# Background work of a two-stage attention and gated-MLP kernel: due times from formulas replaced by a table of places

## The chip, the cores and the metric

The kernel runs on one core of one Trainium2 chip. The metric is the device time of one execution in microseconds (us). It is stated as the median of the runs shown; a profiled execution has its own time.

## The reference

`x` has 4 batches of 12480 rows of 128 numbers; `inducing` has 32 rows. Attention is done twice, first the 32 rows over all rows of a batch, then all rows over the 32 results. What comes out goes through a two-layer network of width 2048 with a gate `h * clip(h + 3, 0, 6) / 6`.

```python
def mab(q, kv):
    s = scale * (q @ kv.transpose(0, 2, 1))
    s = s - s.max(-1, keepdims=True)
    a = np.exp(s)
    a /= a.sum(-1, keepdims=True) + 1e-09
    return a @ kv
h = mab(I, x)                      # I: inducing, once per batch
y = mab(x, h).reshape(49920, 128)
h = y @ w_in                       # 128 x 2048
out = (h * np.clip(h + 3.0, 0.0, 6.0) / 6.0) @ w_out
```

## The kernel before

The kernel doesn't carry every row through the wide network. An output row is a softmax mixture of 32 vectors, so as long as no gate saturates, the network's output is a quadratic form in the 32 softmax weights. Its coefficients are worked out once per batch from the 32 vectors. A check counts at the end whether the conditions held, and a slow direct path would run if not.

The rows of a batch are cut into 7 groups: six of 2048 rows (128 partitions x 16) and a last one of 192 rows (96 partitions x 2). A group of 2048 has four chunks of 512 rows, the last group is one chunk, so a batch has 25 chunks (`NCK`), and the four batches make 100 steps of one loop, `for t in range(total)`.

**A step** makes the output of chunk t. In order: `b_evac` of the chunk before (VectorE multiplies the PSUM tile `op` by `r_all` into `os`, L896; SyncE sends a full group to memory), `b_spread` (SyncE copies `dk` of chunk t+6 to 128 partitions as `d`), `b_prod` (VectorE makes `TD` from `TF` and `d` for chunk t+1, L846), `b_bp` and `b_TF` (TensorE makes `bp` from `xT` and `W`, L818; ScalarE its exponential `TF`, L831; two halves for chunk t+2), `b_lin` (TensorE opens `op` with the linear part from `nf` and `BD`, L857), `b_rp` and `b_r` (the row sums `rp` for t+1, L761, and their reciprocals), and four times `b_quad` (16 matmuls of 128 columns into `op` from `TF`, `TD` and `Cq`, L876).

**Work per group** makes what its chunks need: `b_pp` and `b_dk` (product `pp`, L783, exponential `dk`, L797), `b_ep` and `b_e` (`ep`, L702, and `e`), later `b_sp` and `b_nf` (`sp`, L722, on TensorE; `nf` on VectorE, L732). Before, the first four stand together at one place, seven steps ahead of the group's first chunk (the list `ahead`), and the last two together three steps ahead (`sums`).

**Background work** of the next batch runs between the quads. Phase a, per group: four casts of `xr` to `xb` (`a_cast`, L299), two times eight transposes `pt` (`a_T`, L310) and their copies to `xT` (`a_xT`, L317), scores (`a_scores`, L323), exponential `a` (`a_exp`), two aggregations `hnd` (`a_agg`, L360), and the sum `dacc` (`a_sum`); `load_x` on the queue of GpSimd (POOL) fetches a group of 1 MB into one of five buffers. Phase c: `dred`, `den`, `rD`, `H`, `htp`, `HT`, `W`, `Wd` (from the 32 vectors), `G` (`c_G3`, 48 groups of small products), copies `Gc`, then for each of 16 blocks the differences `dG` on POOL (L543 a gate that reads the latest `TD`, L545 and L546 two subtractions), their square `sq` on ScalarE (L553), and the product `C` (L641) into one long-lived PSUM tile `cp`; also `hs`, `L`, `lt`, `BD` and last `Cq`, which the next batch's quads need.

What sets the order: every engine executes its instructions in the order in which the program issues them (the scheduling is manual). Before, `a_units` and `c_units` give every unit of background work a due time in steps, worked out from weights and a few knots. A sorted `queue` is emptied by `bg` at three places in a step: after quad 0, after quad 1 and the `ahead` entries, and after quad 2. A unit can hold work of several engines: `turned(g, h)` is eight transposes and their copy, `turned(b)` of phase c runs from `htp` to `Wd`. A cast goes to POOL or to ScalarE by a rule; copies `xT` all go to VectorE in the loop. The start of the program, up to the first step, is a list written out by hand (`ORDER`).

PSUM: `bp`, `pp`, `ep`, `sp`, `rp`, `pt`, `s`, `dps`, `htp`, `gp`, `cp`, `lp` and `lt` share five banks (`psF`); `op` has two, `hnd` one. A product that finds no free bank waits until ScalarE or VectorE has read one out.

Of the kernel before, what the change touches and what calls it, by code (L numbers as in the profile page):

```python
# [24 lines left out]
TG = 16  # L25
SL = 4
# [4 lines left out]
CASTLEAD = 1.6  # L31
SUMG = 5
BY_DVE = (2, 6, 11)


# [32 lines left out]
def kernel(  # L68
# [40 lines left out]
    with ExitStack() as es:  # L109
# [44 lines left out]
        held = []  # L154
# [7 lines left out]

        def load_next(b, g):

            if b == 0:
                if g > NGR - XBUF:
                    held.append(g - (NGR - XBUF))
            elif g < XBUF and g + XBUF < NGR:
                load_x(b, g + XBUF)
            elif b + 1 < B:  # L170
                load_x(b + 1, g - (NGR - XBUF))

# [111 lines left out]
        S = {}  # L284

        def a_begin(b):
            S.setdefault(b, {})["dacc"] = cst.tile([P, TG * M], FP32, name="dacc")
# [13 lines left out]
        def a_T(b, g, h, how="f"):  # L301
            t0, p, n = groups[g]
            st = S[b]
            lo, hi = (0, n // 2) if h == 0 else (n // 2, n)
            xb = xbs[(b, g)]
            if h == 0:
                st[("xT", g)] = (xTp if n == TG else xTl).tile([P, n * p], BF16, name="xT")
            pt = bank(how, [P, 1024], BF16, "pt")
            for i in range(lo, hi):
                nc.tensor.transpose(pt[:, (i - lo) * p : (i - lo + 1) * p], xb[:p, i, :], ident_b[:p, :p])  # L310
            st[("pt", g, h)] = pt

        def a_xT(b, g, h, eng):
            t0, p, n = groups[g]
            lo, hi = (0, n // 2) if h == 0 else (n // 2, n)
            pt = S[b].pop(("pt", g, h))
            eng(S[b][("xT", g)][:, lo * p : hi * p], pt[:, : (hi - lo) * p])  # L317
# [35 lines left out]
        def a_agg(b, g, h):  # L353
# [13 lines left out]
            if h and (b, g) != (1, 0):  # L367
                load_next(b, g)
# [9 lines left out]

        def a_units(b, when):

            us = []
            cum = [0.0]

            def put(w, fn, lead=0.0):
                us.append((cum[0], lead, fn))
                cum[0] += w

            def cast(g, h):
                own = h < 2 and when(late_from[g] / cum[0]) >= (b - 1) * NCK
                a_cast(b, g, ((nc.gpsimd.tensor_copy if own else nc.scalar.copy, h, h + 1),))  # L390

            def turned(g, h):
                a_T(b, g, h)
                a_xT(b, g, h, nc.vector.tensor_copy)

            def weighed(g):
                a_scores(b, g)
                a_exp(b, g)

            def summed(g, h):  # L400
                a_agg(b, g, h)
                if h == 0:
                    a_sum(b, g)

            late = []
            late_from = {}
            for g in range(NGR):
                late_from[g] = cum[0]
                k = 1.0 if groups[g][2] == TG else 0.2
                gap = 0.46 * k + (0.49 if late else 0.0)  # L410
                if g == 0 and b > 1:
                    us.append((0.0, CASTLEAD + 0.1, lambda: a_begin(b)))
                if (b, g) == (1, 0):
                    put(0.46 * 2 + 0.2 + 0.5, lambda: None)
                else:
                    for h in range(4):
                        us.append((cum[0] + gap * (h // 2), CASTLEAD - 0.4 * (h % 2), lambda g=g, h=h: cast(g, h)))
                    put(0.46 * k, lambda g=g: turned(g, 0))
                    if late:
                        put(0.49, late.pop(0))  # L420
                    put(0.46 * k, lambda g=g: turned(g, 1))
                    if late:
                        put(0.49, late.pop(0))
                    else:
                        put(0.2, lambda: None)
                    put(0.5 * k, lambda g=g: weighed(g))
                late = [lambda g=g: summed(g, 0), lambda g=g: summed(g, 1)]
                if (b, g) == (1, 0):
                    late = [lambda: load_next(1, 0), lambda: None]
            put(0.4, lambda: None)  # L430
            put(0.1, late[0])
            put(0.1, late[1])
            return [(when(w / cum[0]) - lead, fn) for w, lead, fn in us]
# [225 lines left out]
        def c_units(b, t0, t1):  # L659

            us = []

            def put(at, fn):
                us.append((at, fn))

            def turned(b):
                c_htp(b)
                c_HT(b)
                c_HTb(b, nc.vector.tensor_copy)
                c_HTl(b)  # L670
                c_W(b)
                c_Wd(b)

            put(t0, lambda: c_sum(b))
            put(t0 + 0.9, lambda: (c_den(b), c_rD(b), c_H(b), c_d(b)))
            put(t0 + 1.6, lambda: turned(b))
            put(t0 + 2.7, lambda: c_G3(b, 0, 4))
            put(t0 + 3.05, lambda: c_G3(b, 4, 8))
            put(t0 + 3.4, lambda: c_G3(b, 8, 12))
            put(t0 + 3.75, lambda: (c_G3(b, 12, 16), c_Gcopy(b, 0)))  # L680
            put(t0 + 4.1, lambda: (c_Gcopy(b, 1), c_dG(b, 0), c_dG(b, 1)))
            tb = t0 + 5.0
            pace = (t1 - 1.0 - tb) / FB
            for jb in range(FB):
                at = tb + jb * pace
                put(at, lambda jb=jb: (c_sqG(b, jb), c_dG(b, jb + 2) if jb + 2 < FB else None))
                put(at + 0.99, lambda jb=jb: c_C(b, jb))
            put(t0 + 5.0, lambda: c_hs(b))
            put(tb + 6.5 * pace, lambda: c_L(b, 0))
            put(tb + 7.5 * pace, lambda: (c_L(b, 1), c_Lcopy(b)))  # L690
            put(tb + 10.5 * pace, lambda: (c_lt(b), c_BD(b)))
            put(t1, lambda: c_tail(b))
            return us

# [137 lines left out]

        def b_base(b, c, k):
            b_bp(b, c, k)
            b_TF(b, c, k)
# [219 lines left out]
        queue = []  # L1055

        def bg(at):
            while queue and queue[0][0] <= at:
                queue.pop(0)[1]()

        plan = []

        for b in range(1, B):
            z = (b - 1) * NCK
            knots = {
                1: [(0.0, -3.0), (0.092, -1.0), (0.093, 0.7), (1.0, 9.0)],
                2: [(0.0, z - NCK + 9.5), (0.75, z), (1.0, z + 4.5)],
            }.get(b, [(0.0, z - NCK + 6.0), (0.9, z), (1.0, z + 2.5)])

            def when(f, knots=knots):  # L1070
                for (f0, t0), (f1, t1) in zip(knots, knots[1:]):
                    if f <= f1:
                        break
                return t0 + (t1 - t0) * (f - f0) / (f1 - f0)

            hi = knots[-1][1]
            plan += a_units(b, when)
            plan += c_units(b, hi + 0.4, z + NCK - 1.0)
        queue += sorted(plan, key=lambda u: u[0])
        a_begin(0)  # L1080
        S[1] = {}
# [11 lines left out]
        ahead, sums = {}, {}  # L1093
        for b in range(B):
            for g in range(NGR):
                t = b * NCK + first_chunk[g]
                ahead.setdefault(t - AHEAD - 1, []).append(lambda b=b, g=g: (b_pp(b, g), b_dk(b, g), b_ep(b, g), b_e(b, g)))
                sums[t - LEAD - 1] = (b, g)
# [10 lines left out]
        def counts():  # L1109
            count(1, nf_all[:, :], -1.0e-8, ALU.is_le)  # L1110
            count(2, g_all[:, :], 3.0, ALU.is_le)
            count(6, g_lo[:, :], -3.0, ALU.is_ge)
            count(3, d_all[:, :], 1.0e-20, ALU.is_ge)
            count(4, d_all[:, :], 1.0e30, ALU.is_le)
# [8 lines left out]

        for t in range(total):
# [4 lines left out]
            if evac:  # L1129
                b_evac(*evac)  # L1130
                evac = None
# [12 lines left out]
            op = b_lin(bo, co)  # L1144
            rs = []
            if 0 < t + 1 < total:
# [4 lines left out]
                if k == 2 and rs:  # L1151
                    b_rp(*rs[0])
                    b_r(*rs.pop(0))
            b_quad(bo, co, 0, op)
            bg(t)
            b_quad(bo, co, 1, op)
            for fn in ahead.get(t, []):
                fn()
            bg(t + 0.333)
            if feat:  # L1160
                b_base(fb_, fc, 1)
            if rs:
                b_rp(*rs[0])
                b_r(*rs.pop(0))
            if t == total - 6:
# [165 lines left out]
```

## Time and profile before

| | |
|---|---|
| time, median of 3 runs | 302.05 us (301.92 to 303.36) |
| profiled execution | 302.12 us, span 300.3 us |
| granted TensorE clock | 0.993 |
| TensorE matmul busy | 283.7 us, 94% of the span |
| TensorE weight loads busy | 228.2 us, 76% |
| VectorE, ScalarE, POOL busy | 234.6, 228.5, 116.0 us |
| in the loop: PE's first `op` (L857) to its last | 43.3 to 293.5 us |

PE is TensorE's matmul, PEld its weight load, DVE VectorE, ACT ScalarE, POOL GpSimd, SP SyncE. "Idle <- X" names what ended the wait. A matmul of 128 columns is drawn with its way through the array, so successive ones overlap in the drawing.

### The profile page before, as it was taken

To read this page: it belongs to the slowest core of one execution; us is meant where nothing else is said; L and a number is where in the kernel's file an instruction comes from. 1 tells how busy PE (TensorE), PEld (TensorE's weight loads), DVE (VectorE), ACT (ScalarE), POOL (GpSimd) and SP (SyncE) were. 2 spreads that over 40 slices of the span, in tenths; PEclk is the share of its full clock that TensorE was granted. 3 is DMA by queue.
4 is the path that set the end of the run, shared out by engine and by line. 5 is a ranking of instruction groups with operands and counts; after the bars stand their busy time and mean duration, and the time that the engine had idled before them with its cause. 6 is when DMAs were issued, how large, how long until landed. Compare 5 with 4: busy or idle time off the path is not lost. (4 is left out here: it accounts for less than half of the span.)

```text
span 300.3 us, 9798 instructions
## 1 busy us (share of the span) xinstructions
PE 283.7 (94%) x3950; PEld 228.2 (76%) x3971; DVE 234.6 (78%) x496; ACT 228.5 (76%) x429; POOL 116.0 (39%) x229
## 2 busy tenths in 40 slices
PE   8988999999998999999999999999799999999992
PEld 2778678898887888878888887877578777777881
DVE  1667879878996688879896786787787787888892
ACT  3769988668788988779689888575787787777760
POOL 8374335411049894000396734000877750000000
PEclk9999999999999999999999999999999999999997
DMA  6999399899768269987666515537553656577753
GB/s 207 423 391 257 75 331 407 307 328 347 258 177 288 70 209 309 337 252 259 196 149 235 183 25 189 181 79 213 181 176 75 192 195 214 191 215 219 217 210 111
DMA packets 25281, 66.69 MB, mean 222 GB/s; under 512 B 3184, under 2 KB 18320, under 8 KB 19344
## 3 DMA queue, kind: packets, MB, share of 16 engines
q1 hardware_dynamic: 18784, 38.36, 39.7%
q0 software_dynamic: 6448, 27.66, 29.1%
q8 instruction: 32, 0.52, 0.7%
q14 instruction: 17, 0.14, 0.1%
HBM read 27.67 MB, written 25.56 MB: 177 GB/s over the span
## 5 line engine op out<-in xcount | busy, mean ns | idle before, releaser
L831 ACT ACTIVATE TF<-bp 128x512 bf16<-128x512 f32 (+1 forms) x200 | 115.7, 589 | 33.7 <-PE bp L818 17.7
L876 PE MATMUL op<-Cq,TF 128*128 128x128 bf16 (+1 forms) x784 | 104.6, 221 | 0.3
L876 PE MATMUL op<-Cq,TD 128*128 128x128 bf16 (+1 forms) x784 | 102.5, 219 | 0.0
L896 DVE TENSOR_TENSOR os<-op,r_all 128x512 f32<-128x512 f32 x96 | 65.9, 687 | 22.7 <-PE op L876 22.2
L846 DVE TENSOR_TENSOR TD<-TF,d 128x1024 bf16<-128x1024 bf16 (+1 forms) x100 | 74.6, 746 | 2.5 <-ACT TF L831 1.5
L876 PEld LDWEIGHTS <-TF 128*128 128x128 bf16 (+1 forms) x784 | 55.1, 98 | 24.4 <-issue 12.9
L818 PE MATMUL bp<-xT,W 128*128 128x512 bf16 (+1 forms) x183 | 68.4, 375 | 2.1 <-DVE nf_all L732 1.0
L876 PEld LDWEIGHTS <-TD 128*128 128x128 bf16 (+1 forms) x784 | 60.4, 98 | 0.2 <-issue 0.2
L857 PE MATMUL op<-BD,nf 128*128 128x512 f32 (+1 forms) x100 | 52.5, 525 | 0.0
L299 ACT CAST xb<-xr 128x512 bf16<-128x512 f32 (+1 forms) x67 | 43.9, 663 | 8.0 <-DMA xr<-in_x_dram 7.9
L317 DVE COPY xT<-pt 128x1024 bf16<-128x1024 bf16 (+1 forms) x52 | 31.5, 611 | 15.1 <-PE pt L310 13.8
L546 POOL TENSOR_TENSOR dg<-G 128x256 f32<-128x256 f32 x48 | 40.6, 845 | 0.0
L545 POOL TENSOR_TENSOR dg<-G 128x256 f32<-128x256 f32 x48 | 31.8, 663 | 13.5 <-ACT sq L553 8.8
L543 POOL COPY gate<-TD 128x1 bf16<-128x1 bf16 x48 | 11.7, 244 | 61.2 <-DVE TD L846 60.5
L553 ACT ACTIVATE sq<-dg 128x512 bf16<-128x512 f32 x48 | 30.3, 632 | 3.0 <-POOL dg L546 2.9
L310 PE MATMUL pt<-ident_b,xb 128*128 128x128 bf16 x392 | 30.5, 219 | 1.7 <-POOL xb L299 0.7
L360 PE MATMUL hnd<-xr,a 128*32 128x128 f32 x384 | 30.9, 225 | 0.5 <-ACT a L333 0.5
L310 PEld LDWEIGHTS <-xb 128*128 128x128 bf16 x392 | 23.3, 98 | 5.7 <-POOL xb L299 1.7
L761 PE MATMUL rp<-one,nf 128*128 128x4 f32 (+1 forms) x100 | 26.2, 263 | 0.0
L797 ACT ACTIVATE dk<-pp 128x512 bf16<-128x512 f32 (+1 forms) x28 | 15.6, 557 | 13.7 <-PE pp L783 13.6
L641 PE MATMUL cp<-w_out_b,sq 128*128 128x128 bf16 x256 | 24.3, 219 | 1.5 <-ACT TF L831 1.3
L360 PEld LDWEIGHTS hnd<-xr,a 128*32 128x32 f32 x384 | 24.7, 109 | 1.3 <-ACT a L333 0.6
(125 smaller groups left out, 391.7 us busy)
## 6 DMA issues: line engine op xcount, KB each, us to landing
xr<-in_x_dram POOLq DMA_DIRECT2D x23, 1024.0 KB, 8.6
out_dram<-os SPq DMA_DIRECT2D x23, 1024.0 KB, 4.1
d<-dk SPq DMA_DIRECT2D x96, 128.0 KB, 4.4
xr<-in_x_dram POOLq DMA_DIRECT2D x2, 512.0 KB, 4.7
w_in_r<-in_moe_w_in_dram POOLq DMA_DIRECT2D x2, 512.0 KB, 10.0
w_out_r<-in_moe_w_out_dram POOLq DMA_DIRECT2D x4, 256.0 KB, 10.7
out_dram<-os SPq DMA_DIRECT2D x4, 256.0 KB, 3.5
xl<-in_x_dram POOLq DMA_DIRECT2D x4, 96.0 KB, 4.5
```

The lines of the kernel that those rows point to most:

```text
L299: eng(xb[:p, lo:hi, :], xs[(b, g)][:p, lo:hi, :].bitcast(FP32))
L310: nc.tensor.transpose(pt[:, (i - lo) * p : (i - lo + 1) * p], xb[:p, i, :], ident_b[:p, :p])
L317: eng(S[b][("xT", g)][:, lo * p : hi * p], pt[:, : (hi - lo) * p])
L360: nc.tensor.matmul(st["hnd"][:M, :C], lhsT=st[("a1", g)][:p, i * M : (i + 1) * M], rhs=xs[(b, g)][:p, i, :], start=(g == 0 and i == 0), st ...
L545: nc.gpsimd.tensor_sub(dg[:, 0], stepped(G2, jb, 0, 1, 0), stepped(G2, jb, 2, 0, 2))
L546: nc.gpsimd.tensor_sub(dg[:, 1], stepped(G2, jb, 1, -1, 0), stepped(G2, jb, 10, 0, 2))
L818: nc.tensor.matmul(st[("bp", c, k)][:, :w], lhsT=st["W"][:, k].rearrange("p m i -> p (m i)"), rhs=st[("xT", g)][:, j * w : (j + 1) * w],)
L831: nc.scalar.activation(st[("x", c)][:, k, :w], bp[:, :w], ACT.Exp, scale=scale)
L846: nc.vector.tensor_mul(u[:, :, :w], t[:, :, :w], d[:, :w].unsqueeze(1).to_broadcast([P, 2, w]))
L857: nc.tensor.matmul(op[:p, : S_ * C], lhsT=st[("nf", g)][:R, j * p : (j + 1) * p], rhs=st["BD"][:R, : S_ * C], start=True, stop=False, skip ...
L876: nc.tensor.matmul(op[:p, s * C : (s + 1) * C], lhsT=T[k][:, s * p : (s + 1) * p], rhs=st["Cq"][:, k, :], start=False, stop=(s == S_ - 1 a ...
L896: nc.vector.tensor_mul(ot[:p, j * S_ : (j + 1) * S_, :], op[:p, : S_ * C].rearrange("p (s c) -> p s c", c=C), r_all[:p, b, c, :S_].unsquee ...
```

## The change

The due times, the units, `ahead` and `sums` are gone. A table `PLAN` names every piece of background and group work for the loop, each at a place `@t.k`: step t, place k of 15 in a step. A letter behind a colon names the engine of a cast (`k`) or of a copy to `xT` (`x`): A ScalarE, D VectorE, P POOL. `bg(t, k)` issues what stands at that place. The units are cut to single operations: transposes (`T`) and copies (`x`) apart, scores (`s`) and exponential (`a`) apart, `pp`, `dk`, `ep`, `e`, `sp`, `nf`, `dG`, `sq`, `C` all on their own. Loads (`lx`) have places of their own; they are no longer issued behind the aggregation that frees their buffer.

By the table, 20 casts go to ScalarE, 17 to VectorE and 34 to POOL; of the 40 copies to `xT` of the large and small groups, 15 go to ScalarE and the rest stay on VectorE. The five condition counts that stood together in step 94 (`counts`) are spread over steps 84 to 87 and 98; count 0 stays in step 97. The coefficients `Cq` of batches 1 and 2 are made in steps 25 and 50 ahead of the step's linear part, where they had been due in steps 24 and 49; that of batch 3 is made in step 75, due in 74 before.

```diff
+PLAN = """
+@0.0 k1.1.1:A pp0.2 ep0.4 k1.1.0:D dk0.2 @0.3 ep0.6 e0.6 k1.1.2:D pp0.4 @0.8 T1.1.0 x1.1.0:D k1.1.3:P dk0.4
...
+@10.0 k2.1.0:P k2.1.3:P @10.3 g1.6.0 g1.6.1 @10.5 da1 @10.6 k2.1.1:P T2.1.0 @10.8 lx2.4 H1
+k2.2.2:P nf0.3 x2.1.0:A @10.12 k2.2.0:P @11.2 htp1 HTb1 HT1 Wd1 @11.5 s2.0 a2.0 @11.7 HTl1 @11.12 k2.2.3:A
+ep0.5 pp0.6 @12.0 k2.2.1:A @12.6 e0.5 @13.0 lx2.3 @13.3 G1.0 G1.1 G1.2 G1.3 dk0.6 Gc1.1 Gc1.0 dG1.2 @13.6
+dG1.0 @13.7 T2.2.0 @13.8 x2.2.0:A hs1 g2.0.0 g2.0.1 T2.1.1 x2.1.1:D @13.20 sq1.2 dG1.1 @13.23 sp0.4 @13.28
...
+@24.21 g2.2.0 g2.2.1 @24.22 s2.3 C1.12 k2.5.1:P k2.4.2:D T2.4.1 @24.23 k2.5.2:D sp1.1 a2.3 T2.5.0 g2.3.0 g2.3.1
+T2.5.1 dG1.14 @25.0 x2.4.1:D x2.5.0:D s2.4 @25.1 dG1.7 C1.13 @25.2 nf1.1 @25.3 sp1.2 sq1.14 C1.9 C1.10 @25.4
+x2.5.1:D y2.3 C1.15 sq1.7 C1.7 C1.14 k2.6:P T2.6.1 Cq1 a2.4 y2.4 g2.4.0 g2.4.1 @25.6 lx3.4 @25.12 nf1.2 @25.24
...
+@44.3 g3.1.1 @44.4 g3.2.0 C2.1 pp2.2 @44.5 ep1.6 e1.6 ep2.2 pp2.1 @44.7 e2.2 @44.12 g3.2.1 dk2.2 sq2.8 dG2.12
...
+@56.0 ep2.5 e2.5 pp2.3 dk2.3 @56.2 pp2.4 @56.6 htp3 HTb3 HT3 HTl3 @57.3 G3.0 G3.1 G3.2 G3.3 Gc3.0 Gc3.1 dG3.1
+@57.4 dG3.0 dk2.5 @57.23 dk2.4 @58.4 hs3 @58.8 sp2.4 sp2.3 @58.21 nf2.3 @58.24 sq3.1 @59.8 dG3.5 @59.23 sq3.0
...
+""".split()
-        def load_next(b, g):
...
-        def a_units(b, when):
...
-        def c_units(b, t0, t1):
...
-        def b_base(b, c, k):
-            b_bp(b, c, k)
-            b_TF(b, c, k)
+        def later(kind, b, ix, how):
+            eng = {"A": nc.scalar.copy, "D": nc.vector.tensor_copy, "P": nc.gpsimd.tensor_copy}.get(how)
+            g, h = (ix + [0, 0])[:2]
...
+            elif kind == "T":
+                a_T(b, g, h)
+            elif kind in ("x", "xa"):
...
+                a_xT(b, g, h, eng or nc.vector.tensor_copy)
...
+            elif kind in STAGES:
+                STAGES[kind](b, *ix)
...
+        def bg(t, k):
+            for token in plan.pop((t, k), ()):
+                op, _, how = token.partition(":")
...
+                later(kind + tail, b, ix, how)
...
+        def counts(t):
+            left = total - t
+            if left == 16:
+                count(2, g_all[:, :], 3.0, ALU.is_le)
...
             if evac:
                 b_evac(*evac)
+            bg(t, 0)
+            bg(t, 1)
             if 0 <= t + AHEAD < total:
                 b_spread(*divmod(t + AHEAD, NCK))
+            bg(t, 2)
             if 0 <= tb - 1 < total:
                 b_prod(*divmod(tb - 1, NCK))
+            bg(t, 3)
             if feat:
-                b_base(fb_, fc, 0)
-            if t in sums:
-                b_sp(*sums[t])
-                b_nf(*sums[t])
+                b_bp(fb_, fc, 0)
+            bg(t, 4)
+            if feat:
+                b_TF(fb_, fc, 0)
+            bg(t, 5)
...
             op = b_lin(bo, co)
+            bg(t, 6)
...
             b_quad(bo, co, 0, op)
-            bg(t)
+            bg(t, 8)
             b_quad(bo, co, 1, op)
-            for fn in ahead.get(t, []):
-                fn()
-            bg(t + 0.333)
+            bg(t, 12)
...
```

In the order of PE's instructions, taken from both programs, from the first `op` of the loop on: `sp` stands behind `bp` in all 27 cases before. After, it stands behind a short product (128 columns or fewer) in 22 cases. `op` of L857 stands behind a short product 2 times before, 19 times after; `rp` once before, 10 times after. The products `pp` and `ep` stand in 26 unbroken chains before and 21 after; six of the later chains hold 12 to 20 matmuls, where 8 is the most before.

More of the change, by code (lines that the diff above doesn't have):

```diff
@@ L282, in slots @@
             return min(n, SL), max(n // SL, 1)
-        S = {}
+        S = {b: {} for b in range(B)}
         def a_begin(b):
-            S.setdefault(b, {})["dacc"] = cst.tile([P, TG * M], FP32, name="dacc")
+            S[b]["dacc"] = cst.tile([P, TG * M], FP32, name="dacc")
         def a_cast(b, g, parts):
@@ L377, in a_sum @@
                 nc.vector.tensor_add(dacc, dacc, a1)
-        def a_units(b, when):
[L381 to L433, printed above, removed]
         def c_sum(b):
@@ L657, in c_tail @@
             st["Cq"] = Cq
-        def c_units(b, t0, t1):
[L661 to L693, printed above, removed]
         def b_ep(b, g, how="f"):
@@ L1053, in first @@
                 raise ValueError(kind)
[L1055 to L1078, printed above, removed]
@@ L1079 @@
-        queue += sorted(plan, key=lambda u: u[0])
+        def later(kind, b, ix, how):
+            eng = {"A": nc.scalar.copy, "D": nc.vector.tensor_copy, "P": nc.gpsimd.tensor_copy}.get(how)
+            g, h = (ix + [0, 0])[:2]
+            last = NGR - 1
+            if kind == "k":
+                lo, hi = (0, 4) if g == last else (h, h + 1)
+                a_cast(b, g, ((eng, lo, hi),))
+            elif kind == "T":
+                a_T(b, g, h)
+            elif kind in ("x", "xa"):
+                if g == last:
+                    h = int(kind == "x")
+                a_xT(b, g, h, eng or nc.vector.tensor_copy)
+            elif kind == "s":
+                a_scores(b, g)
+            elif kind == "a":
+                a_exp(b, g)
+            elif kind == "g":
+                a_agg(b, g, h)
+            elif kind == "y":
+                if g == 0:
+                    a_begin(b)
+                a_sum(b, g)
+            elif kind == "lx":
+                load_x(b, g)
+            elif kind == "HTb":
+                c_HTb(b, nc.vector.tensor_copy)
+            elif kind == "G":
+                c_G3(b, 4 * g, 4 * g + 4)
+            elif kind == "L" and ix:
+                c_L(b, g)
+            elif kind in STAGES:
+                STAGES[kind](b, *ix)
+            else:
+                raise ValueError(kind)
@@ new lines @@
+        STAGES = {
+            "dred": c_sum, "den": c_den, "rD": c_rD, "da": c_d, "H": c_H, "htp": c_htp, "HT": c_HT, "HTl": c_HTl,
+            "W": c_W, "Wd": c_Wd, "Gc": c_Gcopy, "hs": c_hs, "dG": c_dG, "sq": c_sqG, "C": c_C, "Lc": c_Lcopy,
+            "lt": c_lt, "BD": c_BD, "Cq": c_tail, "pp": b_pp, "dk": b_dk, "ep": b_ep, "e": b_e, "sp": b_sp, "nf": b_nf,
+        }
+        plan, slot = {}, None
+        for token in PLAN:
+            if token[0] == "@":
+                slot = tuple(int(v) for v in token[1:].split("."))
+            else:
+                plan.setdefault(slot, []).append(token)
@@ L1092 @@
         total = B * NCK
[L1093 to L1098, printed above, removed]
         evac = None
@@ L1107, in count @@
             )
[L1109 to L1114, printed above, removed]
+        def counts(t):
+            left = total - t
+            if left == 16:
+                count(2, g_all[:, :], 3.0, ALU.is_le)
+            elif left == 15:
+                count(6, g_lo[:, :], -3.0, ALU.is_ge)
+            elif left == 14:
+                count(3, d_all[:, :], 1.0e-20, ALU.is_ge)
+            elif left == 13:
+                count(4, d_all[:, :], 1.0e30, ALU.is_le)
+            elif left == 3:
+                count(0, r_flat[:, : NR - SL], 1.0e-16, ALU.is_ge)
+            elif left == 2:
+                count(1, nf_all[:, :], -1.0e-8, ALU.is_le)
         def verdict():
```

93 lines of the change are left out of this document (69 added, 24 removed).

## The prediction

> **What bounds the kernel now.** I read the page's busy times first, then the busy times by stretch, cut where every 25th step opens `op` on L857.
>
> ```profile
> span 300.3 us, 9798 instructions
> PE 283.7 (94%) x3950; PEld 228.2 (76%) x3971; DVE 234.6 (78%) x496; ACT 228.5 (76%) x429; POOL 116.0 (39%) x229
> ```
> ```profile
> L857 PE MATMUL op<-BD,nf x100: 353/582/588, 43.3 to 293.5; 128*128 128x512 f32 x96, 64*96 64x256 f32 x4
> ```
> ```profile
> 0.00:43.30 43.30, 39.48 (x556) 28.63 (x561) 27.15 (x60) 32.01 (x51) 22.70 (x59) 1.00 0.92 276
> 43.30:120.50 77.20, 75.82 (x1161) 64.35 (x1163) 63.48 (x129) 63.91 (x125) 38.04 (x71) 1.00 0.81 274
> 120.50:192.10 71.60, 69.74 (x1019) 57.72 (x1020) 58.59 (x119) 58.65 (x117) 28.35 (x52) 1.00 0.62 195
> 192.10:250.50 58.40, 54.55 (x701) 43.03 (x705) 46.99 (x98) 42.69 (x82) 26.89 (x48) 1.00 0.53 162
> 250.50:294.50 44.00, 43.96 (x526) 34.43 (x529) 37.75 (x91) 31.26 (x57) 0.00 (x0) 1.00 0.68 220
> 294.50:300.30 5.80, 0.15 (x2) 0.04 (x2) 0.63 (x3) 0.00 (x0) 0.00 (x0) 0.62 0.26 90
> ```
>
> The columns are the stretch, its length, then busy time and count of PE, PEld, DVE, ACT and POOL, the granted clock, and the share and rate of the DMA. The loop (second to fifth line) is TensorE's: the clock is full, and the other engines are busy for some 80% or less. PE idles for 77.20 - 75.82 = 1.38, 71.60 - 69.74 = 1.86, 58.40 - 54.55 = 3.85 and 0.04 us: 7.1 us in four batches. The fourth batch, which has no background work, can't be improved by an order at all; the start (43.3) and the end (5.8) hardly change. So the change can move about a fiftieth of the time, and it must take it from these waits. PE's own waits, longest first:
>
> ```profile
> PE cp L641 <- ACT TF L831: 1.3, 1, 1.3
> PE ep L702 <- ACT TF L831: 1.3, 1, 1.3
> ...
> PE htp L471 <- DVE d_all L461: 1.2, 2, 0.8
> PE bp L818 <- DVE nf_all L732: 1.0, 2, 0.8
> PE ep L702 <- DVE nf_all L732: 0.9, 1, 0.9
> PE bp L818 <- ACT dk L797: 0.8, 2, 0.5
> ```
>
> These six (sum 6.5 us, nine waits) are nearly all of the 7.1. Three are waits for a PSUM bank: `ep` or `bp` stands right behind `pp` and `ep` in `ahead`, and ScalarE or VectorE has not yet read an old product out. `cp` waits for a chain: at the third batch the first `sq` on ScalarE stands close behind its `dG`, and holds up the `TF` behind it.
>
> ```profile
> 213.52 0.63 ACT L553 ACTIVATE sq<-dg 128x512 bf16<-128x512 f32 x1 [1.79 <-POOL dg L546]
> ```
>
> **The waits that go.** The table separates what stood together. `pp`, `dk`, `ep` and `e` of a group have places of their own; `H`, `htp` and `G` of batch 3 lie in steps 55.4, 56.6 and 57.3; its first `sq` is at 58.24, most of a step behind the `dG` at 57.3. I take the waits of `ep` (1.3 and 0.9) and `bp` (1.0 and 0.8) as gone, 4.0 us, 1.0 of the 1.3 of `cp` (the 1.79 of ScalarE becomes some tenths), and 0.9 of the 1.2 of `htp`: 5.9 us. What is late next at these places is PE itself. Each wait also hides part of itself, since a matmul of 128 columns is drawn longer than it holds PE:
>
> ```profile
> L876 PE MATMUL op<-Cq,TF 128*128 128x128 bf16 (+1 forms) x784 | 104.6, 221 | 0.3
> ```
> ```profile
> 256.17 0.45 PE op L876 x8
> ```
>
> Eight of them take 0.45, 0.06 each, and each is drawn 0.22 long: 0.16 of each wait is under the drawing. Nine waits make 1.4. Together -7.3 us; the bounds are -9 (all idle time, drawn and hidden) and 0 (they reappear elsewhere).
>
> **What PE pays for the new order.** The matmuls are the same. But `op` on L857, `sp` and `rp` load weights of 4 bytes, which takes long and hides behind the matmul ahead of it:
>
> ```profile
> L857 PEld LDWEIGHTS op<-BD,nf 128*128 128x128 f32 (+1 forms) x100 | 18.9, 189 | 1.9 <-issue 0.8 <-DVE Cq L656 0.2
> ```
> ```profile
> 212.31 0.58 PE L722 MATMUL sp<-e,blk 128*128 128x512 f32 x1
> 212.73 0.39 PE L857 MATMUL op<-BD,nf 128*128 128x512 f32 x1
> ...
> 291.85 0.27 PE L876 MATMUL op<-Cq,TD 128*128 128x128 bf16 x2
> 291.94 0.47 PE L857 MATMUL op<-BD,nf 128*128 128x512 f32 x1
> ```
>
> Behind a product of 512 columns, `op` ends 0.23 after its predecessor (213.12 against 212.89). Behind a short one it ends 0.29 after it (292.41 against 292.12): 0.06 more. By the order of the instructions, `op` goes from 2 short predecessors to 19 and `sp` from 0 to 22: 39 x 0.06 = +2.3 us. `rp` goes from 1 to 10; no row shows that pair, so its price lies between 0 and the whole load of 0.19, and I take 0.1, between the 0.06 and that end: +0.9.
>
> A chain of `pp` and `ep`, which use a quarter of the array's columns at a time, costs something on its way in and out:
>
> ```profile
> 241.53 0.22 PE cp L641 x4
> ...
> 245.71 0.33 PE pp L783 x4
> ...
> 246.26 0.33 PE cp L641 x4
> ```
>
> Four `cp` behind such a chain take 0.33, elsewhere 0.22, and four `pp` at its head 0.33 where side by side a product of 512 columns takes about 0.22: 0.2 for a chain. 21 chains in place of 26: -1.0.
>
> **Engines.** ScalarE, VectorE and POOL change as follows.
>
> ```profile
> L299 ACT CAST xb<-xr 128x512 bf16<-128x512 f32 (+1 forms) x67 | 43.9, 663 | 8.0 <-DMA xr<-in_x_dram 7.9
> L317 DVE COPY xT<-pt 128x1024 bf16<-128x1024 bf16 (+1 forms) x52 | 31.5, 611 | 15.1 <-PE pt L310 13.8
> L299 POOL CAST xb<-xr 128x512 bf16<-128x512 f32 x16 | 10.3, 665 | 17.3 <-DMA xr<-in_x_dram 8.4 <-ACT xb L299 2.7 <-ACT xT L317 2.6
> L317 ACT COPY xT<-pt 128x1024 bf16<-128x1024 bf16 x4 | 4.0, 1008 | 0.5 <-PE pt L310 0.5
> L299 DVE CAST xb<-xr 128x512 bf16<-128x512 f32 x6 | 3.0, 515 | 1.1 <-DMA xr<-in_x_dram 0.9
> ```
>
> Of the casts of 128x512 in the loop 39 leave ScalarE (-39 x 0.663 = -25.9), which takes 15 copies (+15.1): 11 us less of work. VectorE gives these copies (-9.2) and takes 17 casts (+8.8): even. POOL takes 22 casts (+14.6), of its 184 idle us. None of this is a term of the sum, as PE hides it; it says that ScalarE will less often be the one who holds a bank. The loads `lx` keep their distance: POOL reaches each well ahead of its step, and the casts on POOL have only loads and `dG` queued behind them. If one waits for its load, `dG` behind it is late, then `sq`, then `TF`.
>
> **Small terms.** `Cq` of batches 1 and 2 stands in the step that needs it. Two instructions of VectorE then lie between the last `C` and the first quad, behind `nf` and `TD` in the queue:
>
> ```profile
> L654 DVE TENSOR_SCALAR Cq<-cp 128x384 bf16<-128x384 f32 x4 | 2.2, 553 | 0.0
> L656 DVE TENSOR_SCALAR Cq<-cp,half_of 128x128 bf16<-128x128 f32 x4 | 1.4, 342 | 0.0
> ```
>
> PE has transposes, one or two aggregations and `op` as cover, so each costs between 0 and 0.9; I take 0.15 each, nearer the covered end: +0.3. The counts of step 94 spread out:
>
> ```profile
> L1105 DVE TENSOR_SCALAR_CACHE_REDUCE junk<-d_all 128x4 f32<-128x4 f32 x2 | 0.3, 158 | 0.1
> L1105 DVE DVE_READ_ACCUMULATOR junk<-d_all 128x1 f32 x2 | 0.2, 83 | 0.0
> ```
>
> Five of these with their reads are 5 x 0.24 = 1.2 in a step whose slack isn't shown; I give back 0.2 (0 to 0.6, half of them).
>
> **The sum** starts at the profiled execution, 302.12 us (its span and 1.8 around it; the median of the runs is 302.05): 302.1 - 7.3 + 2.3 + 0.9 - 1.0 + 0.3 - 0.2 = **297.1 us**. With the ends of the terms this case reaches from 293 to 300.
>
> **Rivals.** *All idle time goes*, and the new price of the weight loads is lost in waits that remain anyway: 302.1 - 9 - 1.0 = 292. Against it, `htp` and `cp` hang on chains through three engines. Chance 0.08.
>
> *Too few banks; slower.* Six chains of `pp` and `ep` hold 12 to 20 matmuls (steps 22, 27 and 44 among them), so three to five products ask for a bank in a row, while `cp` keeps one of five for most of a batch. Step 24 has a similar pile of three `pt`, `s` and `sp`. The rows above price one such wait at up to 1.3. Two at each of the six chains and at the pile, at 0.9 (the row of `ep` behind `nf`), are 12.6; the sum becomes 309.7, and with two thirds of them 305.5. It decides against the change from the point where about six of the fourteen waits are real (5 us). For it: these very waits carry the loss before. Against it: ScalarE has 11 us less to do and already waits for PE more than PE for it:
>
> ```profile
> ACT dk L797 <- PE pp L783: 13.6, 18, 1.4
> ```
>
> Chance 0.18.
>
> *POOL and VectorE in each other's way.*
>
> ```profile
> L846 DVE TENSOR_TENSOR TD<-TF,d x100: 343/682/1357, 37.8 to 293.1; 128x1024 bf16<-128x1024 bf16 x96, 128x384 bf16<-128x384 bf16 x4
> ```
>
> `TD` takes 0.68 in the median and up to 1.36. If the long ones are those that meet POOL, a share of the 22 new casts will stretch others; the quads wait for `TD`. One in three stretched by half of the difference, 22 / 3 x 0.34 = 2.5, or by a cast's whole 0.665, 4.9, on the path: 297.1 + 3.7 = 300.8. Against it: before, two fifths of POOL's work ran in the loop's first batch, where PE idled least. The Trainium skill, SBUF — State Buffer, section "Who interferes with whom", says that a VectorE instruction with two SBUF inputs and a GpSimd instruction that reads SBUF exclude each other for their whole length, whichever is issued first. It speaks against the 34 casts on POOL, and the maximum of 1.36, twice the median, agrees with it. Chance 0.12.
>
> *Nothing is gained*: the waits move to the next place and the weight loads stay: 302.1 + 0.9 = 303. Chance 0.07.
>
> **The numbers.** My case has 0.55. About 0.5% (1.5 us) is what a measurement can tell from no change: faster is below 300.5, slower above 303.6. Faster: 0.54 of my case, 0.08, and half of the third rival, 0.06: 0.68. Same: the other 0.06, 0.05 of "nothing", 0.04 of the banks and 0.01 of mine: 0.16. Slower: 0.14 of the banks and 0.02: 0.16. The range from 292.0 to 304.5 leaves out some 0.04 below and 0.12 above.
>
> **What would show it.** Right: PE's idle time in the loop near 2 us, no wait of `ep` or `bp` for a bank above 0.5, ScalarE busy for some 10 us less, and `op` and `sp` ending 0.06 later behind short products. Wrong: waits of `ep`, `pp`, `bp` or `pt` for `TF`, `dk`, `e` or `nf` in steps 22 to 27 and 44 (banks); a median `TD` well above the 0.68 of before (POOL); waits of quads for `Cq` in steps 25 and 50, or casts waiting for loads.

## The result, and the profile after

The changed kernel's median is 299.89 us against 302.19 for the kernel before; the ratio is 0.985 [0.981, 0.989]. Its eight executions lie between 295.40 and 301.25, those of before between 301.92 and 303.61. Median and spread count all eight, the ratio leaves out the four longest; the executions from 299.77 us up have a mean granted clock of 0.984 to 0.990, the shorter ones 0.993 to 0.996.

The profiled execution is the shortest of the eight, 295.40 us, 4.5 under the median. The next one took 297.99. Its trace shows what the order does when all goes well; what the other executions lose must come from experiments.

Busy times of the changed kernel, from its page:

```profile
span 293.6 us, 9807 instructions
PE 283.5 (97%) x3971; PEld 227.5 (77%) x3971; DVE 233.8 (80%) x498; ACT 222.8 (76%) x402; POOL 131.8 (45%) x251
```

Busy times by stretch, cut as before at every 25th `op` that opens a step (length, then PE, PEld, DVE, ACT, POOL):

```profile
43.93:122.98 79.05, 78.79 (x1186) 65.92 (x1184) 69.63 (x138) 61.01 (x112) 48.25 (x81) 1.00 0.81 266
122.98:189.14 66.16, 66.11 (x961) 53.91 (x958) 53.19 (x111) 55.64 (x103) 35.39 (x63) 1.00 0.68 223
189.14:245.44 56.30, 56.27 (x750) 44.64 (x748) 46.45 (x100) 43.05 (x82) 25.32 (x48) 1.00 0.52 160
245.44:287.75 42.31, 42.31 (x517) 34.02 (x513) 36.02 (x87) 30.18 (x55) 0.00 (x0) 1.00 0.67 214
```

PE (the matmuls) idles for 0.26, 0.05, 0.03 and 0 us, 0.3 in all instead of 7.1. The four stretches sum to 79.05 + 66.16 + 56.30 + 42.31 = 243.8 us against 251.2. The first is 1.9 longer, since more of the background work and of the group products now lies in it; the three others are 5.4, 2.1 and 1.7 shorter. The last had no idle time to lose: it holds 19 products `pp` and `ep` where it held 35, so 16 of them now lie ahead of it. PE's own waits:

```profile
PE wp L268 <- DVE wake L256: 1.2, 1, 1.2
PE pt L355 <- POOL xb L346: 0.7, 1, 0.7
PE pt L355 <- ACT xb L346: 0.7, 1, 0.7
PE pt L355 <- DVE xb L346: 0.7, 1, 0.7
PE hnd L407 <- ACT a L380: 0.5, 1, 0.5
```

None of the six waits that the prediction named is left. These five rows all belong to the start of the program, before the loop.

### The profile page after: what moved, and what is told of

Same layout as the page of the kernel before. It is cut to its first block, busy times and chain, and to the rows that moved or that the text cites. A ratio compares the mean times of both kernels' runs of the same rounds, so it can differ in the third digit from the quotient of the medians.

```text
span 293.6 us, 9807 instructions
## 1 busy us (share of the span) xinstructions
PE 283.5 (97%) x3971; PEld 227.5 (77%) x3971; DVE 233.8 (80%) x498; ACT 222.8 (76%) x402; POOL 131.8 (45%) x251
## 4 chain that ended last, share of the span: by engine, by line
PE 81%; DMA 6%; DVE 2%; ACT 1%; issue 1%; ACTq 0%; DVEq 0%
PE op L825 29%; PE bp L771 14%; PE op L806 8%; PE hnd L407 6%; DMA d<-dk 6%; PE pt L355 5%; PE cp L630 4%; PE sp L675 3%; PE s L370 2%; PE ep L655 2%; PE pp L736 2%; PE gp L505 1%; PE lp L573 1%; PE dpm L604 1%; PE rp L714 1%; PE lt L589 1%
## 5 line engine op out<-in xcount | busy, mean ns | idle before, releaser
L825 PE MATMUL op<-Cq,TF 128*128 128x128 bf16 (+1 forms) x784 | 100.2, 221 | 0.0
L825 PE MATMUL op<-Cq,TD 128*128 128x128 bf16 (+1 forms) x784 | 98.6, 219 | 0.0
L771 PE MATMUL bp<-xT,W 128*128 128x512 bf16 (+1 forms) x200 | 75.1, 375 | 0.1
L346 POOL CAST xb<-xr 128x512 bf16<-128x512 f32 x38 | 27.8, 742 | 30.0 <-DMA xr<-in_x_dram 12.2
L535 POOL TENSOR_TENSOR dg<-G 128x256 f32<-128x256 f32 x48 | 37.0, 770 | 0.0
L534 POOL TENSOR_TENSOR dg<-G 128x256 f32<-128x256 f32 x48 | 31.6, 659 | 5.1 <-DVE r_all L724 2.3
L355 PE MATMUL pt<-ident_b,xb 128*128 128x128 bf16 (+1 forms) x392 | 29.9, 219 | 2.3 <-POOL xb L346 0.7
L355 PEld LDWEIGHTS <-xb 128*128 128x128 bf16 (+1 forms) x392 | 23.4, 98 | 6.8 <-issue 2.0
L364 DVE COPY xT<-pt 128x1024 bf16<-128x1024 bf16 (+1 forms) x37 | 20.9, 578 | 7.6 <-PE pt L355 7.5
L346 ACT CAST xb<-xr 128x512 bf16<-128x512 f32 (+1 forms) x28 | 20.1, 726 | 7.7 <-DMA xr<-in_x_dram 7.6
L771 PEld LDWEIGHTS <-W 128*128 128x128 bf16 x200 | 19.5, 98 | 5.1 <-issue 4.0
```

The source lines that it names most:

```text
L346: eng(xb[:p, lo:hi, :], xs[(b, g)][:p, lo:hi, :].bitcast(FP32))
L534: nc.gpsimd.tensor_sub(dg[:, 0], stepped(G2, jb, 0, 1, 0), stepped(G2, jb, 2, 0, 2))
L535: nc.gpsimd.tensor_sub(dg[:, 1], stepped(G2, jb, 1, -1, 0), stepped(G2, jb, 10, 0, 2))
L771: nc.tensor.matmul(st[("bp", c, k)][:, :w], lhsT=st["W"][:, k].rearrange("p m i -> p (m i)"), rhs=st[("xT", g)][:, j * w : (j + 1) * w],)
L825: nc.tensor.matmul(op[:p, s * C : (s + 1) * C], lhsT=T[k][:, s * p : (s + 1) * p], rhs=st["Cq"][:, k, :], start=False, stop=(s == S_ - 1 a ...
```

## The experiments

Each one ran in five rounds beside the kernel before, whose medians in the three sets were 302.27 (the first four kernels), 302.44 (the next four) and 302.33 us (the last three). Line numbers in the experiments are one less than in the changed kernel (the unaltered repeat has the same), 13 less where the group products are back, and behind its edit one more than in the kernel before for the one that starts from it.

**The changed kernel again.** The edit is none.

> The changed kernel once more, unaltered, for a second trace: the runs shown of it lie between 295.4 and 301.3 us, those of the kernel before between 301.9 and 303.6. Theory A, a wait of varying length (a transfer that lands late, or a stretch at half clock behind a long wait) is in some executions and not in others: the times spread again over 4 us or more, and a trace of a longer execution shows on TensorE a wait that the 293.6 us trace lacks. Theory B, only the measurement scatters: times within 1.5 us of their median, traces alike.

Measured: median 298.61 us, 295.90 to 300.29 in six executions, ratio 0.989 [0.986, 0.992]. The spread repeats, 4.4 us, and again the profiled execution is the shortest, 2.4 us below the next. So it belongs to the kernel: something in it ends at one time or another, or goes well only beside the profiler, which these two sets can't tell apart.

**The group products back.**

```
+            if t in sums:
+                b_sp(*sums[t])
+                b_nf(*sums[t])
             bg(t, 5)
...
+            if t in ahead:
+                b_pp(*ahead[t])
+                b_dk(*ahead[t])
+                b_ep(*ahead[t])
+                b_e(*ahead[t])
             bg(t, 12)
```

Their entries leave the table; `ahead` and `sums` are filled as before.

> The changed kernel with pp, dk, ep, e, sp and nf put back where they stood before (the first four together seven steps ahead of a group's first chunk, the last two three steps ahead); the rest of the table stays. Theory separation (the prediction's): the bank waits of ep and bp come back, 4.0 us drawn, and the weight loads of sp are covered again, -1.3: 2 to 3 us slower than the changed kernel. Theory engines (the gain comes from the 11 us that ScalarE lost): within 1 us of the changed kernel. Theory chains (the gain comes from den, H, htp and from dG and sq being apart): within 1 us, or 1 us faster by the covered loads.

Measured: 301.12 us (300.65 to 301.68), ratio 0.996 [0.994, 0.997]. Waits that the changed kernel's trace lacks stand among PE's waits in this kernel's:

```profile
PE ep L642 <- ACT TF L771: 1.1, 1, 1.1
...
PE dps L426 <- DVE nf_all L672: 0.6, 1, 0.6
PE cp L617 <- ACT TF L771: 0.5, 1, 0.5
...
PE sp L662 <- DVE nf_all L672: 0.4, 1, 0.4
```

The places of the group products matter; how much, the unsteady times of the changed kernel don't tell yet.

**The engines back.** Of the 71 casts, 60 go to ScalarE and 11 to GpSimd; all copies to `xT` go to VectorE. 64 letters change, such as:

```
-k1.1.0:D ... k2.4.2:D ... k2.5.1:P ... x3.0.0:A ...
+k1.1.0:P ... k2.4.2:A ... k2.5.1:A ... x3.0.0:D ...
```

> The changed kernel with every place kept, but the engines of before: all copies to xT in the loop on VectorE, casts on ScalarE except two of a group of batch 1 and its last group on POOL. Theory separation: engines are off the path, within 1 us of the changed kernel. Theory engines: ScalarE holds banks again, 3 us or more slower than the changed kernel, near or above the kernel before. Theory POOL (casts on POOL stretch TD): 1 to 4 us faster, with TD's mean below the 0.760 of the changed kernel.

Measured: 299.52 us, within 298.87 to 299.87, ratio 0.990 [0.988, 0.992]. PE's first wait in its trace:

```profile
PE pt L354 <- ACT xb L345: 3.4, 6, 0.8
```

ScalarE is late with six casts. On the other hand, with no VectorE cast in the loop, the times lie within 1 us. So the letters for the engines seem to bring something and to cost something.

**`sp` behind `bp`.** 26 of 27 `sp` go to the places 4 and 20 of a step, right behind a `bp`:

```
-@24.8 sq1.15 @24.21 ... @24.23 k2.5.2:D sp1.1 a2.3 ...
+@24.8 sq1.15 @24.20 sp1.1 @24.21 ... @24.23 k2.5.2:D a2.3 ...
```

> The changed kernel with 26 of the 27 products sp moved to the nearest place right behind a bp, so that their 4-byte weight load is covered by 512 columns. Theory weight loads: 22 x 0.06 = 1.3 us faster than the changed kernel. Rival: the load is prefetched anyway or hidden by another wait, no difference beyond 0.5 us.

Measured: 298.12 us, within 297.85 to 298.21, ratio 0.986 [0.983, 0.988]. The time is steady, and now its profiled execution has the loss in it. The tile `xb` in this kernel (count, then shortest, median and longest in ns), and PE, VectorE and POOL in order of time (start, length, and the wait ahead in brackets):

```profile
L345 DVE CAST xb<-xr x23: 368/420/3484, 10.5 to 168.7; 128x512 bf16<-128x512 f32 x23
```
```profile
120.10 1.07 PE L354 MATMUL pt<-ident_b,xb 128*128 128x128 bf16 x16 [1.63 <-DVE xb L345]
```
```profile
116.56 3.48 DVE L345 CAST xb<-xr 128x512 bf16<-128x512 f32 x1
119.96 0.20 DVE L723 RECIPROCAL r_all<-rp 128x8 f32<-128x8 f32 x1
120.08 0.37 DVE L345 CAST xb<-xr 128x512 bf16<-128x512 f32 x1
```
```profile
116.03 1.07 POOL L345 CAST xb<-xr 128x512 bf16<-128x512 f32 x1
117.05 0.18 POOL L531 COPY gate<-TD 128x1 bf16<-128x1 bf16 x1
117.19 0.60 POOL L533 TENSOR_TENSOR dg<-G 128x256 f32<-128x256 f32 x1
117.77 0.66 POOL L534 TENSOR_TENSOR dg<-G 128x256 f32<-128x256 f32 x1
118.38 0.18 POOL L531 COPY gate<-TD 128x1 bf16<-128x1 bf16 x1
118.52 0.60 POOL L533 TENSOR_TENSOR dg<-G 128x256 f32<-128x256 f32 x1
119.09 0.66 POOL L534 TENSOR_TENSOR dg<-G 128x256 f32<-128x256 f32 x1
120.79 0.40 POOL L345 CAST xb<-xl 96x256 bf16<-96x256 f32 x1 [1.03 <-DVE ol L844]
```

A cast of VectorE that takes 0.42 us takes 3.48. It begins while POOL works through its row without a gap, and ends at 116.56 + 3.48 = 120.04, once that row has ended (119.09 + 0.66 = 119.75). Behind it stand the next cast and PE's transposes of step 24, which wait 1.63 us. In the shortest execution of the changed kernel the same cast took 0.89, and seems to have got in between two instructions of POOL:

```profile
115.67 0.89 DVE L346 CAST xb<-xr 128x512 bf16<-128x512 f32 x1
116.55 0.21 DVE L724 RECIPROCAL r_all<-rp 128x8 f32<-128x8 f32 x1
116.67 0.79 DVE L346 CAST xb<-xr 128x512 bf16<-128x512 f32 x1
```
```profile
115.08 1.20 POOL L535 TENSOR_TENSOR dg<-G 128x256 f32<-128x256 f32 x1
116.23 0.80 POOL L346 CAST xb<-xr 128x512 bf16<-128x512 f32 x1
```

There `dg` of POOL is the longer one, 1.20 against 0.66, and no PE waits. So at this place the two engines seem to exclude each other, and which of them gets in first may differ between executions. The Trainium skill, SBUF — State Buffer, section "Who interferes with whom", says that a cast of VectorE can enter a mode that needs the port pair that it shares with GpSimd, and that whoever issues first has the pair for the whole instruction while the other blocks. The rows agree on the exclusion; but 3.48 us is several POOL instructions long, not the rest of one, and over eight times the cast's usual time. The kernels that follow test whether this is the loss.

**All VectorE casts of the loop to ScalarE.**

```
-k1.1.0:D ... k2.4.2:D ... k3.4.0:D      (17 casts)
+k1.1.0:A ... k2.4.2:A ... k3.4.0:A
```

> The changed kernel with all 17 casts that its table gives to VectorE in the loop (mark D) given to ScalarE instead (mark A), each at its place; everything else stays. Theory A, held-up casts: the changed kernel's 5 us between its fastest and slowest executions (295.4 to 301.3) and its median 3 us above the fastest come from VectorE casts that wait out a row of GpSimd instructions, as one did in the run with sp moved (3.48 us instead of 0.42, PE waiting 1.6 us behind it). Then without such casts the times lie within 1.5 us of each other, with a median of 294.5 to 297. Theory B, the spread has another cause (landing of transfers, the clock): the times spread over 4 us as before and the median stays at 298 to 300. Theory C, ScalarE is too late: 17 x 0.73 us more on ScalarE (76% busy) make PE's transposes wait for casts of ScalarE by 3 us or more; then the times are tight, but at 298 to 300.

Measured: 297.62 us, within 297.09 to 297.83, ratio 0.984 [0.982, 0.986]. The times are steady, as theory A expects, but the median is 0.6 above its range. No row shows theory C's long waits for casts of ScalarE, yet many small things are late; its longest waits in the loop are

```profile
PE pt L354 <- ACT dk L749: 0.5, 2, 0.3
PE rp L713 <- ACT xT L363: 0.3, 1, 0.3
PE pt L354 <- ACT xb L345: 0.2, 1, 0.2
```

**Only the two casts of step 24 to ScalarE.**

```
-@24.22 s2.3 C1.12 k2.5.1:P k2.4.2:D T2.4.1 @24.23 k2.5.2:D
+@24.22 s2.3 C1.12 k2.5.1:P k2.4.2:A T2.4.1 @24.23 k2.5.2:A
```

> The changed kernel with only the two VectorE casts of step 24 (k2.4.2 and k2.5.2, which stand between GpSimd's casts and its dG instructions and took 0.89 and 0.79 us in the profile of the changed kernel against 0.42 elsewhere) given to ScalarE. Theory A1, held-up casts, and at this one place: median 295 to 297 and within 2 us, like the run with all 17 moved. Theory A2, held-up casts at several places: median 297 to 298.5, spread half as wide. Theory B, another cause: no difference to the changed kernel, 298 to 300 with over 4 us between the fastest and the slowest.

Measured: 296.11 us, five executions within 296.06 and 296.19, ratio 0.979 [0.978, 0.981]. Two letters of the table bring the median down by 3.8 us from 299.89 (2.5 from the repeat's 298.61) and the spread from 5.9 us (4.4) to 0.13. So the loss had one place. The other 15 VectorE casts do no harm that can be seen here.

**All casts and `sp`.** Two edits from above together:

```
-@24.8 sq1.15 ... k2.4.2:D ... k2.5.2:D sp1.1 ...
+@24.8 sq1.15 @24.20 sp1.1 ... k2.4.2:A ... k2.5.2:A ...   (17 casts, 26 sp)
```

> The 17 VectorE casts given to ScalarE and also 26 of the 27 sp products moved right behind a bp, as in the run with sp moved alone (298.12). Theory A, held-up casts: sp moved removes short products ahead of 4-byte weight loads, some 1.3 us; with the held-up cast gone (1.6 us of PE waiting in that run) this is the fastest of all, 293.5 to 296, and tight. Theory B: no better than the run with sp moved alone, 297.5 to 298.5. Theory C, ScalarE too late: 298 to 300.

Measured: 297.49 us (297.30 to 297.99), ratio 0.985 [0.983, 0.986]: 0.1 from the kernel without VectorE casts. The gain expected of `sp` behind `bp` isn't there.

**One cast in four to VectorE in the kernel before.**

```
-                a_cast(b, g, ((nc.gpsimd.tensor_copy if own else nc.scalar.copy, h, h + 1),))
+                eng = nc.gpsimd.tensor_copy if own else nc.vector.tensor_copy if h == 2 else nc.scalar.copy
+                a_cast(b, g, ((eng, h, h + 1),))
```

> The kernel before with nothing of the change but one cast of four in the loop (part 2 of each group of x, 21 casts) given to VectorE instead of ScalarE. Theory A, held-up casts: VectorE casts beside GpSimd's rows of casts and dG are stretched, the longest to over 1.5 us, and the times spread: over 3 us between the fastest and the slowest, against 2.2 us for the kernel before. Theory B: no difference that can be told, a median of 301.8 to 302.8 within 2 us, or up to 1 us faster since ScalarE has 21 x 0.73 us less to do.

Measured: 303.92 us (303.47 to 305.03), ratio 1.0055 [1.003, 1.008]. It is slower by 1.5 us, but spreads by 1.6 us, not over 3, and no cast is stretched beyond 0.97:

```profile
L299 DVE CAST xb<-xr x23: 409/423/970, 10.1 to 184.3; 128x512 bf16<-128x512 f32 x23
```
```profile
L847 DVE TENSOR_TENSOR TD<-TF,d x100: 348/682/2528, 37.9 to 294.9; 128x1024 bf16<-128x1024 bf16 x96, 128x384 bf16<-128x384 bf16 x4
```

The row has 23 casts against 6 in the kernel before, so 17 moved, not the 21 expected. Both theories' numbers missed. What is held up longest in its loop is a `TD`, 2.53 us, also beside an unbroken row of `dg`. So a VectorE cast is not held up wherever it stands, and casts are not the only victims; where this kernel loses its 1.5 us wasn't tried.

**The two casts and `sp`.**

```
-@24.8 sq1.15 ... k2.4.2:D ... k2.5.2:D sp1.1 ...
+@24.8 sq1.15 @24.20 sp1.1 ... k2.4.2:A ... k2.5.2:A ...   (2 casts, 26 sp)
```

> The kernel with the two VectorE casts of step 24 given to ScalarE (296.11 within 0.13), and also 26 of the 27 sp products moved right behind a bp. The kernel with sp moved alone had 298.12, with one of these casts held up for 3.48 us and PE waiting 1.63 us. Theory A, held-up casts, with the weight loads behind short products costing what the prediction says (0.06 each): 294.5 to 295.3. Theory A without such a price for the weight loads: 295.8 to 296.6, so 1.5 to 2.3 under the kernel with sp moved alone. Theory B, the casts of step 24 are not what held that kernel up: 297.8 to 298.4 as before.

Measured: 296.24 us (295.84 to 296.50), ratio 0.979 [0.977, 0.982]. The two casts take 1.9 us off the kernel with `sp` moved, within what theory A expects without a price for the weight loads. `sp` itself brings nothing measurable (296.24 against 296.11): in the stretches of the loop PE is busy for 0.5 us less (242.5 against 243.0), and idle for 0.5 more, with this wait as the largest in its loop:

```profile
PE sp L674 <- DVE r_all L723: 0.5, 1, 0.5
```

**POOL's row shorter, the VectorE casts left.** The other side of the exclusion:

```
-k2.5.3:P ... k2.5.1:P k2.4.2:D T2.4.1 @24.23 k2.5.2:D
+k2.5.3:A ... k2.5.1:A k2.4.2:D T2.4.1 @24.23 k2.5.2:D
```

> The other side of the same lock: the changed kernel with its VectorE casts left where they are, but two casts of GpSimd's row of steps 23 and 24 (k2.5.3 and k2.5.1) given to ScalarE, so that GpSimd's work without a gap from 113 to 119.7 us is shorter by some 1.5 us and has gaps. Theory A, a VectorE cast waits while GpSimd works without a gap: the times come together, 296 to 297.5 within 1.5 us. Theory B, these two casts are too much for VectorE by themselves, whatever GpSimd does: 298 to 300 and over 3 us between the fastest and the slowest, as in the changed kernel.

Measured: 295.80 us (295.27 to 296.17), ratio 0.978 [0.976, 0.980]: the shortest median of all kernels, 0.2 under theory A's range. The casts stay on VectorE. The first finds the gap that POOL now has; beside the second, it is a `dg` of POOL that is longer, 0.94:

```profile
116.40 0.41 DVE L345 CAST xb<-xr 128x512 bf16<-128x512 f32 x1
117.29 0.21 DVE L723 RECIPROCAL r_all<-rp 128x8 f32<-128x8 f32 x1 [0.48 <-PE rp L713]
117.42 0.37 DVE L345 CAST xb<-xr 128x512 bf16<-128x512 f32 x1
```
```profile
115.26 0.67 POOL L534 TENSOR_TENSOR dg<-G 128x256 f32<-128x256 f32 x1
116.61 0.25 POOL L531 COPY gate<-TD 128x1 bf16<-128x1 bf16 x1 [0.69 <-DVE TD L794]
116.81 0.61 POOL L533 TENSOR_TENSOR dg<-G 128x256 f32<-128x256 f32 x1
117.38 0.94 POOL L534 TENSOR_TENSOR dg<-G 128x256 f32<-128x256 f32 x1
```

So it isn't too much work for VectorE: it is the meeting with POOL's row. Moving either side away gives the same time within 0.3 us.

**The group products back, with the two casts moved.** The group products stand as in the kernel with these back, and two letters change:

```
-k2.4.2:D ... k2.5.2:D
+k2.4.2:A ... k2.5.2:A
```

> The kernel with the group products back at the places of before (301.12) with the two VectorE casts of step 24 given to ScalarE too. It measures the group products' places alone, against 296.11. Theory A with separation: the waits of PE for ep, sp, bp and cp come back as in that kernel, 299.5 to 301, so 3.5 to 5 us for the places; no VectorE cast was held up in that kernel's profile (0.41 and 0.87 us), so little of its 301.12 goes. Theory B, the casts held that kernel up as well and the places are worth little: 297 to 299.

Measured: 300.64 us (300.49 to 301.06), ratio 0.994 [0.992, 0.996], so 4.5 us above the same kernel with the products apart (296.11). Its waits repeat those of the kernel with the group products back:

```profile
PE ep L642 <- ACT TF L771: 1.1, 1, 1.1
...
PE dps L426 <- DVE nf_all L672: 0.7, 1, 0.7
```

The price of the places stands: 4.5 us, and no more than some 0.5 us of that kernel's time (301.12 against 300.64) was due to the two casts.

## Why the prediction was right, and where it was wrong

The forecast was 297.1 us in a range of 292.0 to 304.5, faster. The median is 299.89, inside the range, and faster by 0.8% in the medians, 1.5% in the ratio. The waits went as forecast, and that gives the direction; but the median misses the forecast by 2.8 us, for reasons that the forecast's own case had at nothing. Two of them, a gain and a loss of similar size, nearly cancel, and that the median lies as close as it does is in part luck.

**The waits that go.** Right, and a little larger. Terms of -5.9 drawn and -1.4 hidden were forecast; PE's idle time in the loop fell by 7.1 - 0.3 = 6.8, to be set beside the 5.9. All six waits named are gone, and with the products put back together 4.5 us return. The rival of too few banks is refuted: no wait of `ep`, `pp` or `bp` stands in the list of the changed kernel, and in that of its repeat only one, a `bp` behind `dk`, 0.3 us. Two readings on the way were wrong without harm to the sum: four of the six rows, not three, are waits of `ep` or `bp` (the 4.0 us priced all four), and the fourth batch could get shorter, by 1.7 us, as group products moved ahead of it. The sign "PE's idle time near 2 us" was passed by far.

**What PE pays for the new order.** Mis-sized. The hidden part of the waits, weight loads, chains and the small terms were to sum to -1.4 + 2.3 + 0.9 - 1.0 + 0.3 - 0.2 = +0.9 beside the drawn idle time. The profiled execution took 302.12 - 295.40 = 6.7 us less, and 6.8 of idle time is gone, so these terms sum to +0.1: 0.8 too high. The price per product is there. In the changed kernel, `sp` behind a short product is, for example,

```profile
65.16 0.28 PE L825 MATMUL op<-Cq,TD 128*128 128x128 bf16 x2
65.25 0.47 PE L675 MATMUL sp<-e,blk 128*128 128x512 f32 x1
```

and ends 65.72 - 65.44 = 0.28 after it, where it ended 0.22 to 0.23 behind `bp` in the kernel before. But the term of `sp`, 22 x 0.06 = 1.3, was also tried as a whole: put behind `bp`, it changes the time by -0.1 and +0.1 us in two pairs of kernels. In the second pair PE gets 0.5 us of busy time back, and idles for 0.5 more, the largest wait being that of an `sp` for VectorE. So these 1.3 can't be had back by moving `sp` alone. The terms for `op`, `rp`, the chains and the hidden part weren't tried one by one; which of them makes up the 0.8 is open.

**Engines: "none of this is a term of the sum".** This step failed, twice. The letters that take casts from ScalarE are a gain of 3.4 us: with the engines as before, PE's transposes wait six times for casts of ScalarE, 3.4 us in all, and 299.52 is 3.4 above the 296.11 of the table without the two bad casts. In PE's waits of before, ScalarE's casts held it up for 0.2 us, at the start; but as the other waits go, PE comes earlier to these casts, and they become the next bound. So the -5.0 us that the sum gave to the order alone measure 2.8 without the new engines (302.27 - 299.52). And the same letters lose 2.5 to 3.8 us by the medians to one meeting of VectorE with POOL, in step 24. Of that, some 2 us are the meeting itself: the pair of kernels with `sp` moved gives 1.9, and the changed kernel's executions that weren't profiled and had a granted clock of 0.993 or 0.994, 297.99 to 298.83 in both sets, lie 1.9 to 2.7 above 296.11. The third rival named the right two engines and was close in time (300.8), but by luck: it spread the price over 22 POOL casts, stretching some of the `TD` by 0.34 to 0.67. Median `TD` is 0.681 (0.682 before); the price is a single cast of VectorE held up for over 3 us. The rule of the Trainium skill that it quoted was about instructions with two inputs; the cast has one. The sign of ScalarE came out at half: its busy time fell by 228.5 - 222.8 = 5.7 us, not by some 10.

**Small terms.** No wait for `Cq` stands among PE's waits of the changed kernel, and casts that waited for their loads held up no one there; 0.3 and 0.2 are below what the runs can tell.

By its own case, without the meeting, the prediction would have been 1.0 to 1.3 us too high (297.1 against 296.11 and 295.80). Parts don't simply add: the places without the new engines give 2.8 us, the rest of the table with the new engines, but without the group products' places, 302.33 - 300.64 = 1.7, both together, without the meeting, 302.44 - 296.11 = 6.3.

What stays open. No trace shows a long execution of the changed kernel itself: both profiled ones were the shortest of their sets. So no execution without the profiler is known to have gone well, and the profiler may take part in who wins. That the cast is held up in the long ones is inferred, from the trace with `sp` moved and from the two kernels in which moving either side of the meeting ends the spread. Nor is it settled why the seven longest executions of both sets, 299.68 us and more, have a lower granted clock (0.984 to 0.990); the kernel before has 0.989 in 4 of its 36 executions beside the experiments, 303.00 to 303.95 us against 301.59 to 302.69 for the others, and in the two kernels without the meeting the clock stayed at 0.992 to 0.997. These two ran on another chip than the repeat of the changed kernel; the kernel before agrees between the chips within 0.2 us, which makes the chip an unlikely cause, but the changed kernel wasn't repeated beside them.

## What to carry to other kernels

When an order takes away the waits in front, ask which engine's queue was next late behind them: here the casts on ScalarE, worth 3.4 us, stood in the list of before with 0.2 us. Where a table puts VectorE work beside a long row of GpSimd work without a gap, look at the longest instruction of its line, not at the median, and leave a gap in one of the two rows where TensorE stands behind. And if times spread by 2% while the profiled execution is the shortest, one thing to suspect is that two engines compete for something. Move one of them: here the spread went when the right one was moved.

## What the hardware showed

- A VectorE cast of 128x512 that takes 0.42 us in the median took 3.48 beside a row of POOL instructions, and did not get in between one POOL instruction and the next for 3 us. In the shortest execution of the changed kernel it took 0.89. In another kernel a `TD` took 2.53 us beside such a row, against 0.68 in the median.
- With a gap of 0.69 us in POOL's row, the same two casts took 0.41 and 0.37 us, and beside the second a `dg` of POOL took 0.94 against 0.67.
- The product `sp`, whose weights have 4 bytes, ended 0.28 us after a short product and 0.22 to 0.23 after one of 512 columns. Moving 26 of them behind products of 512 columns didn't change the time by more than 0.1 us.
- Executions of one program lay between 295.4 and 301.3 us while this meeting was in it, and within 0.13 us once two casts were moved. That the winner of the meeting differs from one execution to the next is inferred.
